# A retention layer and its feed-forward block: the second chunk's recurrence by halves of 64 tokens, with other orders of loads, activations and PSUM tiles

## The chip, the cores and the metric

The kernel runs on one core of one Trainium2 chip. The metric is the device time of one execution in microseconds (us). TensorE (PE) does the matmuls, VectorE (DVE) and ScalarE (ACT) the work on elements, GpSimd (POOL) a few small operations, and SyncE (SP) issues nearly all transfers (DMA), in one queue that is served in order: an instruction that waits holds those behind it.

## The reference

```python
# q, k, v: (B, H, S, D) = (4, 8, 768, 64), fp32
gamma = 1.0 - 2.0 ** (-5.0 - np.arange(H))
for t in range(S):
    state = gamma[None, :, None, None] * state + np.einsum('bhd,bhe->bhde', k[:, :, t], v[:, :, t])
    y[:, :, t] = D ** -0.5 * np.einsum('bhd,bhde->bhe', q[:, :, t], state)
x = y.transpose(0, 2, 1, 3).reshape(3072, 512)
h = x @ w_in                   # (512, 2048)
out = np.maximum(0.01 * h, h) @ w_out      # (2048, 512)
```

The two weight matrices arrive as 64-bit floats and are turned into fp32 on the chip.

## The kernel before

**Chunks.** The 768 tokens are cut into six chunks of `C = 128`; a chunk holds the 128 tokens of all four batches, so 512 rows of x. Decay is taken out of the recurrence: v is multiplied by `gk` ahead of it (`decay_v`, on ACT in the first two chunks, on POOL later) and the result by `gq` behind it (`next_gq` moves `gq` on by one chunk), so that the state itself is a plain sum of k v^T.

**The recurrence in the first two chunks** goes batch by batch over 128 tokens. `score` makes q k^T for the 128 tokens (only the three of four 64 x 64 quarters that are not zero), `masked` (DVE, L211) multiplies by the mask, `reads` (L226) multiplies q with the state, `last_values` and `first_values` (L261, L250) add the scores times v, `state` (L276) makes the new k v^T in the same PSUM tile, `taken` (DVE, L306, L312) copies the result to x times `gq` and adds to the state. In the second chunk two batches go together (`products_together`), and batch 1's scores lie in two banks of the feed-forward pool (`score_apart`, `masked_apart`).

**The recurrence from the third chunk on** (`c >= JOINED`, 2) goes by pairs of batches and by halves of 64 tokens. `scores_of_pair` makes the scores within each half (L369) and the sums k v^T of each half (L380), then on DVE two masked tiles `am` (L387), the state after the first half, `mid`, and the state after the second (both L606, by `plus`). `joint_visit` reads the old state for the first half and `mid` for the second (L427) and adds the scores times v (L444); two POOL memsets (`rows_free`) order matmuls that share rows of the array; four DVE copies (L466) take the result to x, batch 1 of the pair first. For the third chunk both are put between steps of the feed-forward block (`early_scores`, `early_visit`), in a PSUM pool `psum` with two slots of two banks.

**Layout of loads.** Host code lays k and v out token by token; from chunk `JOINED` on, one transfer brings k of both batches of a pair and another v of both (`of_pair`, kind 0 and 1). Tiles with tag "qk" and tag "kv" have two buffers each (`AHEAD`). The last four weight pieces, 28 to 31, use the same buffers for their raw words: even ones "qk", odd ones "kv".

**Feed-forward, first two chunks.** `direct` (L683), `hidden` and `output` (L662) multiply by seven products of 2 x 2 blocks. Each product, and each step of `direct`, is four fp32 matmuls of 128 x 256, which the profile shows as a row of x8: every fp32 matmul is two records. The seven go through four PSUM banks A to D, M1 being copied into bank B by ACT; `differences` makes the sums of x blocks that the products need (t[0] first), `add_sums` and `last_sum` those of the weights. Between the steps the 32 pieces of weights are turned into fp32: `powers` on ACT (three activations), `mantissas` on DVE (L590, L595, L602). `sum_of_unit` and `keep_unit` prepare further sums of weights and store them (`kept`).

**Feed-forward, later chunks.** From 240 us on, `inner` (L1182) does a second level of seven products with the stored weights, read back into `wa` and `wb` (`load_unit`, group 0 and 1), and `outer` puts its results together on DVE and applies the leaky activation on ACT (L1218). `inner` copies products to SBUF on ACT (L1186 to L1194): M3 adds into the bank that held M5, M7 into the one that held M6, so each waits for that copy.

**Order.** The order on each engine is the order of the Python calls (`tc.manual_schedule()`); waits come from the tile framework. Steps of a product are interleaved by hand: `run(steps, {2: [...]})`, `next(steps)`, `products(steps, n)`, and the tables `hidden_more` and `output_more`, whose key `s3` means "after step 3".

## Time and profile before

| | us |
|---|---|
| profiled execution | 644.66 |
| its span, first to last instruction | 642.9 |
| six runs: 644.66, 645.28, 646.89, 642.82, 642.52, 642.72; median | 643.74 |
| PE busy in the span | 631.7 (98%) |
| DVE busy | 462.6 (72%) |
| ACT busy | 269.5 (42%) |
| POOL busy | 22.7 (4%) |

A row of the timeline gives the start, the busy time, the engine, the source line, the operation, the tiles written and read, the tile of the array, the shape and the number of records; a bracket tells how long the engine stood before and what ended that. A windows row gives for a stretch the busy time of each engine, then the granted clock of TensorE (1.00 is full), the busy share of the DMA engines and what they moved in GB/s. Ends of matmuls are modelled, so the distance of two starts is a better measure than a busy time.

### The profile page before, as it was taken

The page shows a single profiled execution, that of the slowest core. Times are in us where ns is not written, and L with a number is a line of the kernel's source. Part 1 is how long each engine was busy: PE and PEld are TensorE (multiplying, and loading weights), DVE is VectorE, ACT ScalarE, POOL GpSimd, SP SyncE. Part 2 cuts the span into 40 slices and gives each one's busy share as a digit, 9 for nine tenths or more (in the row PEclk, how much of TensorE's full clock was granted, in tenths as well). Part 3 has the DMA queues.
Part 4 walks back from the last instruction along what each step waited for, and adds up shares of the span by engine and source line. Part 5 has one row for each costly group of instructions (what it writes and reads, how often), then busy time and mean ns, then how long its engine had stood idle before and what let it go on. Part 6 is the DMA issues. An engine that isn't in the chain of part 4 may idle for free.

```text
span 642.9 us, 14287 instructions
## 1 busy us (share of the span) xinstructions
PE 631.7 (98%) x6086; PEld 570.6 (89%) x6086; DVE 462.6 (72%) x760; ACT 269.5 (42%) x515; POOL 22.7 (4%) x45
## 2 busy tenths in 40 slices
PE   8999999999999989999999999999999999999997
PEld 5888888888888879899999999999999999999996
DVE  5689769889979856657876756778637778637655
ACT  5876557257252114352342433523424423533521
POOL 2000000000011010101000001000010000000000
PEclk9999999999999989999999999999999999999999
DMA  8931327455953987384844573844445336545201
GB/s 332 406 120 46 119 66 246 129 198 157 308 220 92 354 308 260 88 295 127 275 133 136 165 228 110 296 161 156 152 151 190 95 115 187 166 150 167 86 1 67
DMA packets 87536, 113.42 MB, mean 176 GB/s; under 512 B 3240, under 2 KB 71720, under 8 KB 87472
## 3 DMA queue, kind: packets, MB, share of 16 engines
q1 hardware_dynamic: 87168, 111.88, 52.7%
q8 instruction: 48, 0.79, 0.5%
q10 hardware_dynamic: 304, 0.62, 0.3%
q14 instruction: 16, 0.13, 0.1%
HBM read 93.35 MB, written 19.14 MB: 175 GB/s over the span
## 4 chain that ended last, share of the span: by engine, by line
PE 88%; DMA 6%; DVE 3%; ACT 2%; issue 1%; SPq 0%; DVEq 0%
PE bank L662 31%; PE bank L1182 27%; PE B_o L662 4%; PE C_o L662 4%; PE A_o L662 4%; PE A_h L662 3%; PE C_h L662 3%; PE B_h L662 3%; DMA qk<-in_qk_dram 2%; PE D_o L662 2%; PE D_h L662 2%; DMA x_words<-in_weights_dram 1%; DMA in<-in_kv_dram 1%; PE bank L444 1%; PE bank L380 1%; PE bank L369 1%
## 5 line engine op out<-in xcount | busy, mean ns | idle before, releaser
L606 DVE TENSOR_TENSOR o<-o,bank 128x512 f32<-128x512 f32 (+2 forms) x91 | 58.6, 662 | 55.0 <-PE bank L662 33.5
L606 DVE TENSOR_TENSOR made<-made,bank 128x512 f32<-128x512 f32 (+1 forms) x96 | 56.4, 619 | 57.0 <-PE bank L1182 52.6
L662 PE MATMUL bank<-g,w 128*128 128x256 f32 x384 | 89.9, 382 | 0.0
L662 PEld LDWEIGHTS bank<-g,w 128*128 128x128 f32 x384 | 70.7, 190 | 9.2
L1182 PEld LDWEIGHTS bank<-x,wb 128*128 128x128 f32 x672 | 77.6, 192 | 0.8
L1182 PE MATMUL bank<-x,wb 128*128 128x128 f32 x672 | 77.6, 275 | 0.0
L1182 PE MATMUL bank<-x,wa 128*128 128x128 f32 x512 | 68.8, 276 | 0.6 <-ACT made L1188 0.6
L662 PE MATMUL bank<-gd,w 128*128 128x256 f32 x288 | 66.1, 379 | 0.0
L1182 PEld LDWEIGHTS bank<-x,wa 128*128 128x128 f32 x512 | 63.8, 192 | 2.4 <-ACT bank L1186 0.8
L662 PEld LDWEIGHTS bank<-gd,w 128*128 128x128 f32 x288 | 54.7, 190 | 7.4
L1182 PE MATMUL bank<-t,wa 128*128 128x128 f32 x384 | 53.3, 275 | 0.0
L1218 ACT ACTIVATE g<-g 128x512 f32<-128x512 f32 x64 | 39.5, 632 | 31.5 <-DVE g L606 31.5
L1182 PEld LDWEIGHTS bank<-t,wa 128*128 128x128 f32 x384 | 48.0, 192 | 0.0
L1186 ACT COPY bank<-bank 128x512 f32<-128x512 f32 (+1 forms) x32 | 16.7, 522 | 67.8 <-PE bank L1182 67.5
L606 DVE TENSOR_TENSOR g<-made 128x512 f32<-128x512 f32 x64 | 42.7, 688 | 1.1
L755 ACT COPY bank<-bank 128x512 f32<-128x512 f32 x17 | 9.7, 570 | 72.4 <-PE bank L662 72.3
L609 DVE TENSOR_TENSOR gd<-g,gd 128x512 f32<-128x512 f32 x48 | 33.2, 692 | 4.9
L773 ACT COPY bank<-bank 128x512 f32<-128x512 f32 x16 | 9.1, 570 | 50.2 <-PE bank L662 50.2
L662 PE MATMUL bank<-g,last 128*128 128x256 f32 x120 | 29.0, 387 | 0.0
L662 PE MATMUL bank<-gd,last 128*128 128x256 f32 (+1 forms) x124 | 27.5, 373 | 0.0
L662 PE MATMUL A_h<-x,w 128*128 128x256 f32 x112 | 26.6, 380 | 0.0
L662 PEld LDWEIGHTS bank<-gd,last 128*128 128x128 f32 x124 | 22.8, 190 | 3.2 <-DVE gd L609 0.3
(223 smaller groups left out, 1030.5 us busy)
## 6 DMA issues: line engine op xcount, KB each, us to landing
wa<-kept SPq DMA_DIRECT2D x16, 1344.0 KB, 8.0
raw<-in_weights_dram SPq DMA_DIRECT2D x31, 512.0 KB, 4.3
wb<-kept SPq DMA_DIRECT2D x16, 896.0 KB, 5.3
wa<-kept SPq DMA_DIRECT2D x16, 448.0 KB, 4.3
wb<-kept SPq DMA_DIRECT2D x16, 448.0 KB, 6.2
out_dram<-o SPq DMA_DIRECT2D x23, 256.0 KB, 3.3
kept<-w SPq DMA_DIRECT2D x12, 448.0 KB, 5.8
qk<-in_qk_dram SPq DMA_DIRECT2D x10, 512.0 KB, 8.2
```

What stands on the lines that cost most here:

```text
L369: nc.tensor.matmul(at[j][ts(h, 64), n, m, i], lhsT=x[ts(j, 64), 1, a, ts(h, 64)], rhs=x[ts(j, 64), 0, a, ts(h, 64)], start=(n == 0 and a = ...
L380: nc.tensor.matmul(sums[h][ts(j, 64), n, a], lhsT=key[ts(h, 64), 2 * a + j], rhs=val[ts(h, 64), 2 * a + j], start=(n == 0 and a == 0), sto ...
L444: mm = nc.tensor.matmul(at[n][j][ts(i, 64), m, ts(h, 64)], lhsT=val[ts(h, 64), 2 * a + j], rhs=weights[j][ts(h, 64), n, m, i], start=(n == ...
L606: nc.vector.tensor_tensor(out=out, in0=a, in1=b, op=ALU.add)
L609: nc.vector.tensor_tensor(out=out, in0=a, in1=b, op=ALU.subtract)
L662: nc.tensor.matmul(to, lhsT=block(w, sa)[:, k, ts(i, 128)], rhs=rhs[:, k, a:z], start=(first and (i == 0 or split) and n == 0 and k == 0), ...
L755: nc.scalar.copy(out=bank_of("B"), in_=ps)
L773: nc.scalar.copy(out=bank_of("D"), in_=ps)
L1182: nc.tensor.matmul(ps[q][:, i], lhsT=w[:, j, i], rhs=part_of(moving[i], s), start=(i == 0 and m in ("M1", "M5", "M4")), stop=True, skip_gr ...
L1186: nc.scalar.copy(out=ps[3], in_=ps[0])
L1218: nc.scalar.activation(g[:, i], g[:, i], AF.Prelu, alpha=0.01)
```

## The change

**Second chunk.** `JOINED` becomes 1, so the second chunk's k and v come by pairs and its recurrence runs through `early_scores` and `early_visit`. `reads`, `score_apart`, `masked_apart`, `products_together` and `scored_later` go. The places where `c > JOINED` stood now read `c > 2`. For each pair the tile with v is loaded ahead of the one with k, and v of both batches is decayed ahead of the pair's sums.

**Loads.** The third chunk's two qk loads move ahead of its v and k; the fourth chunk's likewise, and `load_unit(0, 1)` (`wb`) moves behind them.

**PSUM tiles.** `early_visit` asks for the tile of batch 1 of the pair before that of batch 0.

**Activations.** At the start of the two-level part, `outer(0, 1)` runs its DVE sums ahead of the last output step, and its four leaky activations come in twos after M1 and after M4 of the next inner product instead of all four after M1.

```diff
+    def inputs_into(place, c, b, kind):
+        flat = place.rearrange("p i k n -> p (i k n)")
+        half = 2 * HP * C
+        heads[c, b + kind] = [flat[:, 0:half].rearrange("p (s a t) -> p s a t", s=2, a=HP)]
+        load_qk(c, b + kind)
+        of_pair(c, b, kind, flat[:, half : 2 * half].rearrange("p (n h d) -> p n h d", n=2, h=H))
+        rooms[c, b, kind] = flat[:, 2 * half : 2 * half + 2 * HP * D]
...
     def early_visit(c, b):
         def do():
-            joint_visit(c, b, [pair_of_banks(f"yp{n}_{c}_{b}") for n in range(2)])
+            banks = [pair_of_banks(f"yp{n}_{c}_{b}") for n in (1, 0)]
+            joint_visit(c, b, banks[::-1])
         return do
...
+            load_qk(2, 0)
+            load_qk(2, 1)
             of_pair(2, 0, 1)
             of_pair(2, 0, 0)
-            for b in range(2):
-                load_qk(2, b)
...
-    load(1, 0, unit_tile(LATE[2], "in10"))
-    load(1, 1, unit_tile(LATE[1], "in11"))
+    inputs_into(unit_tile(LATE[2], "in11"), 1, 0, 1)
+    inputs_into(unit_tile(LATE[1], "in10"), 1, 0, 0)
...
-    load(1, 2, unit_tile(LATE[0], "in12"))
+    inputs_into(unit_tile(LATE[0], "in13"), 1, 2, 1)
...
-    load(1, 3)
+    heads[1, 2] = [work.tile([128, 2, HP, C], FP32, tag="qk", bufs=AHEAD, name="qk_1_2")]
+    load_qk(1, 2)
+    of_pair(1, 2, 0)
...
     next(steps)
-    scored_later(0)
     decay_v(1, 1, nc.scalar)
+    early_scores(1, 0, spare(1, 0, 0))()
+    next_powers()
     next(steps)
-    score_apart(1, 1)
-    next_powers()
-    next_mantissas()
-    for j in range(2):
-        masked_apart(1, 1, j)
-    next_powers()
-    products_together(0)
+    early_visit(1, 0)()
     next_mantissas()
     decay_v(1, 2, nc.scalar)
+    decay_v(1, 3, nc.scalar)
     next_powers()
-    decay_v(1, 3, nc.scalar)
-    taken(1, 0, x1)
-    taken(1, 1, x1)
     next(steps)
-    scored_later(2)
-    scored_later(3)
+    early_scores(1, 2, spare(1, 2, 1))()
+    next_mantissas()
     later = hidden(1, 0, x1, t1, *parts[1][1:], order=FIRST)
     next(later)
     last_sum(0)
+    next_powers()
+    early_visit(1, 2)()
     next_mantissas()
-    products_together(2)
     next_powers()
     run(steps, {})
-    tokens_taken(1, 2, x1)
-    tokens_taken(1, 3, x1)
     differences(x1, t1)
     next_gq()
-    state_taken(1, 2, for_state(sums_at[1, 2]))
-    state_taken(1, 3, for_state(sums_at[1, 3]))
...
         load_unit(0, 0)
...
-        load_unit(0, 1)
 
     def next_heads():
+        for b in range(2):
+            ahead(3, b)
         of_pair(3, 0, 1)
         of_pair(3, 0, 0)
-        for b in range(2):
-            ahead(3, b)
...
-                     s3=[early_visit(2, 0), differ(2), next_heads],
+                     s3=[early_visit(2, 0), differ(2), next_heads, lambda: load_unit(0, 1)],
...
     inner(0, 1)
+    later = []
+    outer(0, 1, later)
     products(last, 1)
     begun = inner_steps(1, 0, held=True)
-    products(begun, 1)
-    outer(0, 1)
+    for steps, leakies in ((1, later[:2]), (2, later[2:])):
+        products(begun, steps)
+        for do in leakies:
+            do()
...
-                products(begun, 7)
+                products(begun, 5)
...
-JOINED = 2
+JOINED = 1
```

## The prediction

> **What bounds the kernel now.** I read the page first: TensorE (PE) is busy 98% of the span and the chain that ended last is 88% PE, so only PE's own work and PE's waits count; VectorE (DVE, 72%) and ScalarE (ACT, 42%) matter where PE waits for them. The windows give PE no idle time from 35 to 200 us. So in the second chunk each microsecond of matmuls is one of time. Next the timeline of PE alone. Columns: start, busy, engine, line, tiles, records; every fp32 matmul is two records.

> ```profile
> 25.74 1.89 PE L683 MATMUL d<-x,w 128*128 128x256 f32 x8
> 27.56 0.90 PE L191 MATMUL ap<-in 64*64 64x128 f32 x32
> 28.39 1.99 PE L683 MATMUL d<-x,w 128*128 128x256 f32 x8
> ...
> 44.64 1.99 PE L683 MATMUL d<-x,w 128*128 128x256 f32 x8
> ...
> 48.20 1.03 PE L662 MATMUL C_h<-t,w 128*128 128x256 f32 x4
> ```

> ```profile
> 190.07 1.89 PE L662 MATMUL A_h<-x,w 128*128 128x256 f32 x8
> 191.89 1.16 PE L369 MATMUL ap<-in 64*64 64x64 f32 x64
> 192.87 1.11 PE L380 MATMUL sp<-in,in 64*64 64x64 f32 x64
> 193.92 1.99 PE L662 MATMUL C_h<-t,w 128*128 128x256 f32 x8
> ...
> 199.20 1.89 PE L662 MATMUL A_h<-x,w 128*128 128x256 f32 x8
> ...
> 203.19 1.13 PE L662 MATMUL C_h<-x,w 128*128 128x256 f32 x4
> ```

> The upper rows are the ends of the second chunk's recurrence, which stands between dense blocks; the lower ones are the third chunk's, already by halves: scores and state sums of a pair at 191.89, its visit between 199.20 and 203.19. The distance of two dense starts, less a dense block's 1.73 us, is what an excursion costs, with the gaps where the tile shape changes.

> Then PE's waits. After 186 us the same timeline shows five, and the windows show what one of them does to the clock:

> ```profile
> 209.12 0.69 PE L369 MATMUL ap<-qk 64*64 64x64 f32 x32 [0.48 <-DVE x L466]
> 210.69 0.69 PE L369 MATMUL ap<-qk 64*64 64x64 f32 x32 [0.88 <-DMA qk<-in_qk_dram]
> ...
> 233.99 0.69 PE L369 MATMUL bank<-qk 64*64 64x64 f32 x32 [1.55 <-DMA qk<-in_qk_dram]
> 235.24 0.69 PE L369 MATMUL bank<-qk 64*64 64x64 f32 x32 [0.56 <-DMA qk<-in_qk_dram]
> ...
> 259.86 0.49 PE L1182 MATMUL bank<-x,wa 128*128 128x128 f32 x2 [0.59 <-ACT made L1188]
> ```

> ```profile
> 236.00:240.00 4.00, 4.00 (x71) 3.53 (x66) 2.65 (x4) 0.00 (x0) 0.00 (x0) 0.60 0.41 91
> ```

> The windows row is a stretch, the engines' busy times, and as its last three numbers the granted clock, the DMA share and GB/s: 0.60 after PE stood 2.1 us. Last, SyncE's (SP) own timeline, for why qk was late:

> ```profile
> 202.81 0.33 SPq L136 DMA_DIRECT2D k<-in_kv_dram  x1
> 203.18 1.72 SPq L119 DMA_DIRECT2D qk<-in_qk_dram  x2
> ```

> The qk loads stand behind k, whose room comes free late. 22 us later it is the same again: wb is issued at 219.44, v at 221.55 (its issue took 3.71), k at 225.36 and only then qk at 225.78.

> **Part 1, the second chunk by halves.** From the dense block at 25.74 to C_h at 48.20 before: 22.46 us, of which six dense blocks (25.74, 28.39, 35.41, 38.83, 44.64, 46.48) are 6 x 1.73 = 10.38 and the filling of bank B some 0.32 (38.83 to 40.97, less the 1.82 from block to recurrence). That leaves 11.76 for two pairs. By halves a pair costs 193.92 - 190.07 - 1.73 = 2.12 for scores and sums and 203.19 - 199.20 - 1.73 = 2.26 for the visit (2.12 at 215.81 to 219.66): 4.31, twice 8.62. Ideal gain 3.14. Against it stand new waits:
> - The sums of pair 0 need both batches' decayed values. ACT decays the second from 27.61 to 29.63, behind two leaky activations and next_gq as before; the sums reach it at 28.96 and would end at 29.43, so they end near 29.8: 0.4 lost. Queued behind them on PE is only the dense block.
> - Loads: the order in SP is the same in bytes. Values come first (landed 23.4), the last keys are issued at 18.21 and 24.77; transfers into these tiles landed 7.0 to 10.1 us after issue, so by 28.3 and 34.9, and are needed at 28.5 and 36.5. Cost 0, up to 0.3. ACT decays pair 2 in one go from 31.5 to 35.6, before its sums.
> - DVE: am, am and two states take 2.52 (195.27 to 197.79), the four copies of a visit 1.32 (207.60 to 208.92), a weight piece's mantissas 1.86 (30.88 to 32.74). The first visit ends near 33.8 and from there DVE runs without a gap: copies to 35.0, mantissas to 36.9, pair 2's am and states to 39.4, mantissas to 41.3, last_sum to 41.9, copies to 43.2, mantissas to 45.0 (now ahead of the differences), t[0] to 45.7. C_h wants t[0] at 45.5, so it starts near 45.85, not 45.06 as without any wait: that is 2.35 before 48.20. The states need 39.7 for the second visit, which starts at 39.7: no wait, at most 0.3.
> - The lag of DVE meets one copy of bank B near 58 us: 0.15. DVE's idle time at 69.12 and 74.42 (0.98 and 2.15, waiting for PE and ACT) then gives the rest back, so the lead stays to 186 us, and DVE's chain from 188.61 starts from PE's C_h.
> Taken: 2.2; ends 0.3 (pairs wait 2.8 us more) and 3.1.

> [...] The rows decide: 128 records of the visit at 201.02 to 203.19 take 2.17 us, 17 ns each.

> **Part 2, the third chunk's loads.** At 209: qk(2,0) takes the room of weight piece 28 and is issued before 185.6; qk(2,1) that of piece 30, free at 198.95, some 4 us earlier than now. What they are moved past: v(2,0) now waits behind qk(2,1), is issued near 199.4 rather than 185.56, and with 3.4 to 4.7 us to land is there by 204; POOL's decay (2.54) ends by 206.6, the sums need it at 209.5. The 0.48 goes too: early_visit now takes its banks so that those copied out first, 0.7 us before the others, are the ones the next scores need. So A_o at 206.75 plus 1.73 plus 2.12 gives C_o at 210.60 instead of 212.25: 1.65. Ends 0.9 (only the load's wait goes) and 1.9.

> At 234: qk(3,0), qk(3,1), v, k now stand ahead of wb and are issued as soon as the visit ends (218, on the clock of before less part 1), ahead of wb's 1344 KB. The kept stores ahead of them lose two qk transfers (3.4 us). Behind wa (issued by 214, then 8.0 to landing on the page, so 222) and at 1.3 us per 512 KB (382 to 406 GB/s in the windows from 230 to 236), qk lands by 225, v by 226.5, POOL's decays (2.04) end by 228.6; the scores start at 230.7, the sums 0.9 later. wb lands 4 us after k, near 231.7; its first matmul, 248.23 before, moves to 242.5. The five stores of o follow wb instead of qk; the loads into o's room wait for them and are needed only at 269. Without the wait the dense block at 230.55 is followed by 2.12 of excursion and a block of 1.73 at full clock: L1182 starts at 236.13 instead of 240.25: 4.12. Of this some 1.6 is the halved clock (sums 1.81 for 0.93, dense block 2.67 for 1.92 in the chain of waits). Ends 2.1 (the clock still drops) and 4.2.

> [...] Here 2.1 us of standing sufficed, while 1.36 us at 209 to 211 left 1.00. [...]

> **Part 3, the leaky activations.** At 258.11 ACT runs them ahead of the copy that M3 waits for (0.59). Now two follow M1's copy and two M4's; M5's copy ends at 258.0, M3 wants it at 259.1. M6's copy ends near 260.25, M7 wants it at 260.0. So 0.59 becomes 0.2: 0.4 gained, ends 0 and 0.6. DVE's add into o moves behind five sums; its bank is not written before 269, and the output's transfer has no reader.

> **Sum.** 2.2 + 1.65 + 4.12 + 0.4 = 8.4. The profiled execution took 644.66 (span 642.9, 1.8 around it): 636.3. It lies 0.9 above the median of the six, 643.74; if the waits for qk make that spread, as I take it, the result comes from 636.3, else from 635.4.

> **Rivals.**
> - DVE eats part 1. For: it is without a gap from 34 to 46 in my working, and a mantissa step of 1.86 us now stands ahead of t[0]. Against: its recurrence is no larger (8.2 us in the rows before, 2 x 3.84 = 7.7 after). Part 1 falls to 0.3: 638.2.
> - The late load of the fourth chunk moves, but stays: qk and v wait behind kept and wa, v's decay ends 2 us after the scores want to start, and the clock halves as before. For: v took 9.9 us to land. Against: 3 us of margin above. Part 2 falls to 1.65: 640.4.
> - Slower: the sums of a pair stand in PE's order before a dense block and need both batches' loads and sixteen decays by ACT. If the second pair's loads or ACT come late, PE stands us for us, and beyond 2.1 us the clock adds 1.6. For: DMA is 96% busy to 35 us. From 6.8 us of standing the run is slower than before; with 10 us it is 644.66 - 8.4 + 11.6 = 647.9. Against: pair 2's values are issued at 20.92 and so there by 31.0, 0.5 before ACT asks for them.
> - The change doesn't do what it says: the order of instructions shows the quarters, loads and activations where the diff has them; left out.

> **How the numbers follow.** Forecast 0.65, DVE 0.18, late load 0.13, slower 0.04. The low end, 634.0, is the upper ends of all parts (9.8) off the median of the six; the high end, 640.2, leaves out the slower case and most of the late load. A change of 0.5% (3.2 us) is about what a measurement can tell: faster 0.92 (forecast, DVE and nearly all of the late load), same 0.05, slower 0.03.

> **What would show it.** C_h's start near 45.9 (right) or above 47.5 (DVE); no PE wait for qk near 207 and 227; clock 1.00 between 225 and 240; no wait for ACT's copy above 0.3 near 252. A PE wait above 1 us for anything in 27 to 45 us, or for v or wb near 228 to 245, makes it wrong.

## The result and the profile after

| | before | after |
|---|---|---|
| median of the runs side by side, us | 644.52 (47 runs, 642.13 to 648.05) | 640.00 (21 runs, 639.08 to 641.92) |
| ratio | | 0.9934, 95% interval 0.9922 to 0.9947 |
| profiled execution, its span | 644.66, 642.9 | 640.17, 638.4 |
| start of C_h in the second chunk | 48.20 | 49.24 |
| start of L1182, L1126 after | 240.25 | 235.92 |

By the ratio the kernel is 0.66% faster, by the medians 4.5 us, where 8.4 were forecast. The 640.0 lies inside the range, at its upper end. The page of the kernel after, its engines' line, one of its DMA queues, and the chain that ended last:

```profile
PE 629.5 (99%) x6214; PEld 568.1 (89%) x6214; DVE 462.5 (72%) x763; ACT 269.4 (42%) x515; POOL 22.7 (4%) x45
...
q8 instruction: 49, 0.80, 0.5%
...
PE 96%; DMA 1%; DVE 1%; ACT 1%; issue 1%; SPq 0%; DVEq 0%
```

DMA's share of the chain falls from 6% to 1%, and the waits for qk are gone. The second line becomes important below (packets, MB, share); before it read:

```profile
q8 instruction: 48, 0.79, 0.5%
```

The later stages of PE's timeline, for the rows before at 209 to 240, and the windows for the clock:

```profile
207.95 1.89 PE L628 MATMUL A_o<-g,last 128*128 128x256 f32 x8
209.77 1.16 PE L334 MATMUL ap<-qk 64*64 64x64 f32 x64
211.81 1.99 PE L628 MATMUL C_o<-gd,last 128*128 128x256 f32 x8
...
231.93 1.16 PE L334 MATMUL bank<-qk 64*64 64x64 f32 x64
235.92 0.38 PE L1126 MATMUL bank<-x,wa 128*128 128x128 f32 x2
```

```profile
235.00:240.00 5.00, 5.00 (x43) 4.87 (x42) 3.46 (x7) 2.57 (x5) 0.00 (x0) 1.00 0.66 213
```

Scores in one row without a bracket: no wait for qk at either place, and the clock is 1.00. But the second chunk is late. Its rows, and all the waits of PE there that are new:

```profile
24.00 0.46 PE L238 MATMUL yp<-am,in 64*64 64x64 f32 x16 [0.66 <-issue]
...
28.04 1.16 PE L334 MATMUL ap<-in 64*64 64x64 f32 x64
...
29.02 0.65 PE L345 MATMUL sp<-in,in 64*64 64x64 f32 x31
...
31.44 0.73 PE L345 MATMUL sp<-in,in 64*64 64x64 f32 x33 [1.76 <-issue]
32.10 1.99 PE L649 MATMUL d<-x,w 128*128 128x256 f32 x8
...
44.23 0.40 PE L392 MATMUL yp<-in,states 64*64 64x64 f32 x12 [0.63 <-issue]
...
49.24 1.10 PE L628 MATMUL C_h<-t,w 128*128 128x256 f32 x4 [0.20 <-ACT dec L100]
```

"issue" says that PE stood and the profile shows nothing that it waited for. The first stands in the last rows of the first chunk, ahead of the recurrence that was changed; the other two stand in the middle of a group of equal matmuls, the longest after 31 of the 64 records of pair 0's sums. ACT's decays, which the prediction named for that place, were over at 30.10; PE went on at 31.44. A bracket with "issue" on the engine that bounds the kernel is the thing to follow.

**What PE waited for.** q8 carries instructions, by its name on the page. It made 49 fetches of 16.4 KB (16,384 bytes each in the trace; 0.80 MB in all). The trace has 12,428 matmuls and weight loads and 94 other instructions of TensorE: 12,522 / 49 is 255.6 for each fetch, so 256 with the last one not full, 64 bytes an instruction. Before it was 12,263 in 48, 255.5. So I take q8 to bring PE's own instructions in blocks of 256. In order of start, with its semaphore instructions, those ahead of which PE stood are the 706th, 962nd and 1730th: 256, and three times 256, apart. So each is the first of a block. The same count holds in every profile of this case: PE stood 0.25 us or more without a releaser 26 times between its first and its last matmul, in eleven profiled executions, and each time the instruction behind the wait is the 194th plus a multiple of 256. No other wait of that length is without a releaser. The DMA view of the kernel after shows when the block that began at 31.44 was fetched. From 24.00, where the block ahead of it began, to 28.9 the engines are full (DMA share 1.03) and q8 has no packet; then it has its one:

```profile
DMA packets 550, 2.02 MB, mean 412 GB/s; under 512 B 57, under 2 KB 57, under 8 KB 550
...
q1 hardware_dynamic: 550, 2.02, 103.3%
```

```profile
q8 instruction: 1, 0.02, 5.7%
```

The first fence is 24.0 to 28.9, the second a row of 28.9 to 30.1. The trace puts the fetch at 28.99 and its end at 30.09; PE went on 1.35 us after that. The same reading for the other two waits: fetch ended at 22.64, PE on at 24.00 (1.36); 42.92 and 44.23 (1.30). So theory F: a block of 256 is fetched at about the time when PE comes to the block ahead of it; the fetch stands behind the loads that fill the DMA engines (it began 5.0 us here after PE began the block ahead; 0.66 and 1.03 behind 285.88 and 35.31, where the DMA share was 0.00); 256 short matmul instructions, 128 records, last 2.2 us (the visit at 202.23 to 204.40 takes 2.17), so the next block isn't there. In the kernel before, PE began the block ahead at 23.52; the fetch ended at 29.56, so by the 1.35 above the next block could be used at some 30.91. PE, with its 128-token matmuls, was through the block ahead only at 31.59: 0.7 us of margin that nobody saw.

### The profile page after: what moved, and what is told of

It reads as the page before. It is cut to its first block, busy times and chain, and to the rows that moved or that the text cites. A ratio compares the mean times of both kernels' runs of the same rounds, so it can differ in the third digit from the quotient of the medians.

```text
span 638.4 us, 14552 instructions
## 1 busy us (share of the span) xinstructions
PE 629.5 (99%) x6214; PEld 568.1 (89%) x6214; DVE 462.5 (72%) x763; ACT 269.4 (42%) x515; POOL 22.7 (4%) x45
## 4 chain that ended last, share of the span: by engine, by line
PE 96%; DMA 1%; DVE 1%; ACT 1%; issue 1%; SPq 0%; DVEq 0%
PE bank L628 32%; PE bank L1126 27%; PE C_h L628 4%; PE B_o L628 4%; PE A_o L628 4%; PE C_o L628 4%; PE B_h L628 4%; PE A_h L628 4%; PE d L649 2%; PE D_o L628 2%; PE D_h L628 2%; DMA raw<-in_weights_dram 1%; PE bank L334 1%; PE bank L409 1%; PE bank L392 1%; PE bank L345 1%
## 5 line engine op out<-in xcount | busy, mean ns | idle before, releaser
L1126 PEld LDWEIGHTS bank<-x,wb 128*128 128x128 f32 x672 | 77.6, 192 | 0.8
L1126 PE MATMUL bank<-x,wb 128*128 128x128 f32 x672 | 77.6, 275 | 0.0
L1126 PE MATMUL bank<-x,wa 128*128 128x128 f32 x512 | 68.7, 276 | 0.1
L1126 PEld LDWEIGHTS bank<-x,wa 128*128 128x128 f32 x512 | 63.8, 192 | 1.8 <-ACT bank L1130 0.8
L1126 PE MATMUL bank<-t,wa 128*128 128x128 f32 x384 | 53.4, 275 | 0.0
L1168 ACT ACTIVATE g<-g 128x512 f32<-128x512 f32 x64 | 39.4, 632 | 30.8 <-DVE g L572 30.8
L1126 PEld LDWEIGHTS bank<-t,wa 128*128 128x128 f32 x384 | 48.0, 192 | 0.0
L628 PE MATMUL bank<-g,last 128*128 128x256 f32 x120 | 28.3, 380 | 0.0
```

Source lines behind the costliest of these rows:

```text
L628: nc.tensor.matmul(to, lhsT=block(w, sa)[:, k, ts(i, 128)], rhs=rhs[:, k, a:z], start=(first and (i == 0 or split) and n == 0 and k == 0), ...
L1126: nc.tensor.matmul(ps[q][:, i], lhsT=w[:, j, i], rhs=part_of(moving[i], s), start=(i == 0 and m in ("M1", "M5", "M4")), stop=True, skip_gr ...
L1168: nc.scalar.activation(g[:, i], g[:, i], AF.Prelu, alpha=0.01)
```

## The experiments

Rivals to F: A, the sums wait for decayed values or loads; D, DVE's chain bounds the second chunk; R, chance; later T, transfers of one kernel.

**The parts alone.** The first is the kernel before with the second and third part of the change, its second chunk as it was; in the other only the second chunk is changed. Lines of the first one's edit:

```diff
+            banks = [pair_of_banks(f"yp{n}_{c}_{b}") for n in (1, 0)]
+            joint_visit(c, b, banks[::-1])
...
+            load_qk(2, 0)
+            load_qk(2, 1)
             of_pair(2, 0, 1)
             of_pair(2, 0, 0)
...
+        for b in range(2):
+            ahead(3, b)
         of_pair(3, 0, 1)
         of_pair(3, 0, 0)
...
+    later = []
+    outer(0, 1, later)
```

> The kernel before with the second and third part of the change alone (order of loads, PSUM tiles, leaky activations); its second chunk's recurrence stays as before. Theory F (part 1 costs time, because PE's instructions are fetched too slowly for its short matmuls; parts 2 and 3 gain what was forecast): 1.65 + 3.9 + 0.25 = 5.8 us faster than before, so about 638.5 us and faster than the changed kernel by 1.2 us. Rival D (part 1 gains as forecast and the loss lies in later stages): 6 us less gain than that here, or about 642 us, slower than the changed kernel.

638.88 us, ratio 0.9942 (0.9926 to 0.9958). The trace: C_h 48.24, A_o 206.76, C_o 210.62, L1182 234.78, with no PE wait above 0.4 from 14 us on. As F says.

> The changed kernel with the second and third part undone, so that only the second chunk's recurrence by halves is left. Theory F: PE waits in the sums of pair 0 (1.8 us) and in the visits without any releaser, C_h starts near 49.2 us, and the kernel is 1 us slower than before, 645.5. Rival D: C_h starts near 46 and the kernel is 2 us faster, 642.5.

644.89 us beside 643.32 of before, ratio 1.0025 (1.0002 to 1.0049): part 1 alone costs time. The profiled execution was the slowest of twelve, 650.21. The waits of 1.76, 0.62 and 0.48 are at the same matmuls. C_h starts at 50.39, later than expected: the clock was 0.50 from 33 to 35 us after the wait of 1.76, which it was not in the profiled execution of the change.

**Fewer loads under way.** In the trace of the change SP lets each load wait for the eighth before it (the one at 17.12 for that of 7.39, by their semaphore); here for the third or the second, from the second chunk's first load to its last.

```diff
+    def paced(load):
+        if len(issued) >= 3 and pacing[0]:
+            tc.add_manual_dep(load.ins, issued[-3].name, IN_ORDER, reason="pace of the loads")
+        issued.append(load.ins)
...
-        nc.sync.dma_start(out=raws[n], in_=weights[n])
+        paced(nc.sync.dma_start(out=raws[n], in_=weights[n]))
```

> The changed kernel, in which each of SP's loads of the second chunk and of the weight pieces between them waits until the third load before it has landed, so that at most three are under way. Theory F with its cause (an instruction fetch of PE stands behind the transfers that are queued in the DMA engines, 5.0 us at 24 us): the fetches at 21.5 and 29.0 start 1 to 2.5 us earlier, the waits of 0.66 and 1.76 shrink to 0 to 0.5 together, one of up to 1 us may come in the first visit, and C_h starts near 47.5 to 48; 1 to 2 us faster than the changed kernel. Rival A (the wait in the sums is for ACT's decays or for the pair's loads): loads land no earlier or later, so the wait stays at 1.8 us or grows, and the time is that of the changed kernel or longer.

> As the run before, with at most two loads under way. Theory F: the fetches start earlier still (delay 1.3 to 2.5 us behind the block's first instruction), no wait in the sums of pair 0; but the loads may lose bandwidth and land 1 to 3 us later, which PE would then wait for by name (DMA) in pair 1 or in the pieces' conversion. Rival A: later loads make the wait in the sums longer than 1.8 us.

The fetch behind 23.3 us starts 2.5 us after PE began the block ahead with three loads under way and 1.7 with two, instead of 5.0. Both kernels have no wait on "issue" left in the second chunk. PE's rows with three:

```profile
27.35 1.16 PE L343 MATMUL ap<-in 64*64 64x64 f32 x64
28.33 1.46 PE L354 MATMUL sp<-in,in 64*64 64x64 f32 x64
...
33.66 1.99 PE L658 MATMUL d<-x,w 128*128 128x256 f32 x8
36.88 0.69 PE L343 MATMUL ap<-qk 64*64 64x64 f32 x32 [1.23 <-DMA qk<-in_qk_dram]
...
38.96 1.34 PE L354 MATMUL sp<-in,k 64*64 64x64 f32 x64 [0.92 <-DMA k<-in_kv_dram]
...
48.33 1.97 PE L637 MATMUL C_h<-t,w 128*128 128x256 f32 x8 [0.21 <-DVE t L584]
```

The sums of pair 0 come in one row of 64. A falls: the loads land later and the wait goes all the same. But the DMA engines are no longer full (80% busy from 23.3 to 25.7 us), pair 1's qk and k come late, and PE now waits for them by name. 639.25 us, ratio 0.9946 (0.9931 to 0.9961). C_h comes 0.91 us earlier than in the change; in all 1 to 2 us were expected, and the gain is not shown: the median is 0.75 us lower, but the two were not run side by side, and the changed kernel's ratio is 0.9934. With two loads qk is 5.98 us late: 647.48 us.

**The change again, and other queues.** Four loads under way, and both depths with weight piece 6 loaded behind pair 1's qk and k.

```diff
-        if n != 3:
+        if n not in (2, 3):
             load_piece(n + 4 if n < 3 else n + 3)
...
     of_pair(1, 2, 0)
+    load_piece(6)
```

> The changed kernel again, beside the next three. Theory F: the waits of 0.66, 1.76 and 0.63 without a releaser are there again within 0.2 us, since the position of the instruction blocks and the queued transfers are the same; about 640 us. Rival R (these waits are chance): they are elsewhere or of another length.

> The changed kernel with at most four loads under way until the second chunk's last one is issued (three starved the DMA engines: pair 1's qk and k came 1.2 and 0.9 us late). Theory F: the fetch behind 24 us starts 2.5 to 4 us after the block's first instruction instead of 5.0; the wait in the sums of pair 0 is 0 to 1.0 us, pair 1's loads come in time or up to 1 us late; C_h near 47.5 to 48.5, 638.5 to 639.5 us.

> At most three loads under way as in the run with three, and piece 6 of the weights is loaded behind pair 1's qk and k instead of ahead of them (1.3 us each earlier). Theory F: no wait without a releaser in 23 to 33 us; the waits of 1.23 for qk and 0.92 for k shrink to 0 to 0.4; C_h near 46.4 to 47.2, where the forecast's own sum would have it but for the loads; 637.3 to 638.5 us, faster than before, than the changed kernel and than the kernel with the second and third part alone. Rival D (DVE's chain bounds part 1): C_h stays at 48 or later, with a wait for t, although PE stands no more ahead of it.

> The same order with at most four loads under way. Theory F: waits without a releaser of up to 1 us, no wait for qk or k; C_h near 46.4 to 47.5; 637.3 to 638.8 us.

| run | waits on "issue", 23 to 46 us | other waits for loads | C_h | C_h less these waits | median us |
|---|---|---|---|---|---|
| the change, profiled | 0.66, 1.76, 0.63 | | 49.24 | 46.19 | 640.00 |
| the change again | 1.76, 0.31, 0.36 | | 48.87 | 46.44 | 639.96 |
| three loads | none | 1.23, 0.92 | 48.33 | 46.18 | 639.25 |
| four loads | 1.22, 1.13, 0.27 | | 49.18 | 46.56 | 640.69 |
| three, other order | 1.00, 1.52 | | 48.82 | 46.30 | 640.27 |
| four, other order | 0.68, 1.49, 1.13, 0.44 | | 50.03 | 46.29 | 640.94 |

The wait of 1.76 is not chance: it is there again to 0.01 us, though the 0.66 is gone, the 0.63 is 0.36, and 0.31 in the first visit is new. The three kernels with other queues stood 1.2 to 2.1 us above the upper ends of their expected times: once the second pair's loads are in time, PE comes to the next block sooner and stands there (at 39.76, in pair 1's sums, with three loads and the other order). In these runs a wait for instructions that was shortened in one place came back in the next. A pair is two blocks (256 records, 512 instructions), and from PE's start of one block to the use of the next it took 7.4 us in the change while the engines were full (24.00 to 31.44: 5.0 + 1.10 + 1.35); with idle engines some 3 is an estimate (0.66 + 0.92 behind 285.88, and the 1.35 from above). In all of these the wait for instructions ended 1.2 to 1.7 us after the fetch's last byte.

**The blocks moved, nothing else.** 64 more instructions in front, at 2 us.

```diff
-    keep_busy(10)
+    keep_busy(7)
+    for _ in range(35):
+        nc.tensor.matmul(idle[:, 0, 0:64], lhsT=nothing, rhs=nothing[:, 0:64], start=True, ...)
```

> The changed kernel with 64 more TensorE instructions in front (35 narrow matmuls on zeros for three of the ten wide ones that keep PE busy at 2 us), so that every block of 256 instructions begins 64 earlier in the program. Theory F: the wait that came after 31 of the 64 records of pair 0's sums comes ahead of the first of them (62 instructions earlier) and lasts 0.8 to 1.7 us; the one in the second visit moves from the middle of a group of reads to a place 64 instructions ahead, in the values or the first reads; the first visit gets one of 0.5 to 2 us. Together they stay near 2.5 us, and so does the time, 640 us within 1. Rival A (the wait is for decayed values or loads): it stays at the same matmul, after 31 records.

```profile
28.70 1.23 PE L345 MATMUL sp<-in,in 64*64 64x64 f32 x64
...
34.83 0.38 PE L409 MATMUL yp<-am,in 64*64 64x64 f32 x9 [2.00 <-issue]
```

The data are the same, and the sums of pair 0 run through, where 0.8 to 1.7 us of waiting ahead of them were expected: PE began the block ahead 1.6 us earlier (22.37 for 24.00), the fetch ended at 27.07, so by the 1.35 above the block could be used at some 28.4; the sums began at 28.70. The wait is now in the first visit, 2.00 us, 64 instructions ahead of where the change has its next block. The second visit has no wait above 0.25, where one was expected. A is out for good. The time, 640.75 us, stays within 1.

**Fewer bytes.**

```diff
+        if n in (4, 5, 6):
+            nc.gpsimd.memset(raws[n].bitcast(U32)[:, 64:], 0)
+            nc.sync.dma_start(out=raws[n][:, 0:32], in_=weights[n][:, 0:32])
+            return
```

> The changed kernel with a sixteenth of the bytes of weight pieces 4, 5 and 6 loaded (the rest of their words is set to zero on POOL), which takes some 3.7 us of transfers out of the stretch from 22 to 33 us. Theory F: the fetch that started 5.0 us after its block's begin starts within 3.5; the waits without a releaser between 23 and 36 us shrink from 2.1 to 0.6 or less in sum; C_h starts at 46 to 46.8 instead of 49. Rival D: C_h stays above 47.5 and waits for DVE or ACT.

> The kernel before with the same three pieces cut to a sixteenth, as a control. Theory F: nothing to gain, C_h stays at 48.2 within 0.3, so that the run with the change is ahead by 1.4 to 2.2 us at C_h, the forecast of part 1 (2.2). Rival D: C_h moves as far as in the run with the change, and part 1 gains nothing even so.

A miss: 638.95 us (ratio 0.9925) with the change, 644.80 (1.0017) without. With the change the fetch still starts 4.82 us after PE began the block ahead and PE still stands 1.64 and 0.45; C_h is at 48.00. SP issued the loads of the chunk no earlier than in the changed kernel (the last, k, at 25.18 for 24.35), and the engines were still full from 24 to 28 us (DMA share 1.06 in the windows), when the fetch was waiting; only from 28 to 32 did the share fall, to 0.41. So this run doesn't test part 1 without contention, as it was meant to, and why fewer loads under way shorten the fetch's wait while fewer bytes did not is left open. C_h of the control stayed, at 48.27, but the lead of 1.4 to 2.2 us at C_h that was expected over it is 0.27.

**Half of it, and the same half with other blocks.** Pair 0 by whole batches as before, pair 1 by halves; then the same with 80 instructions in front (`keep_busy(7)` and 43 narrow matmuls).

```diff
-    early_scores(1, 0, spare(1, 0, 0))()
...
-    early_visit(1, 0)()
+    scored_later(0)
...
+    products_together(0)
...
+    taken(1, 0, x1)
+    taken(1, 1, x1)
```

> The changed kernel with pair 0 of the second chunk (batches 0 and 1) by whole batches as before, and pair 1 alone by halves; second and third part of the change as they are. Theory F: pair 0 needs 352 instructions less... of the short kind than by halves only in part, but its fetches had a margin of 0.7 us before, so no wait above 0.3 there; pair 1 stands after the loads have landed and its second visit waits 0 to 0.6; C_h at 46.8 to 47.7; 637.3 to 638.5 us, faster than before, than the changed kernel, and than the kernel with the second and third part alone. Rival D: C_h at 48 or later.

> The mixed kernel (pair 0 by whole batches, pair 1 by halves) with 80 more TensorE instructions in front, so that each block of 256 begins 80 earlier; nothing else differs. Theory F: the wait of 1.00 at 45.1 and that of 4.40 at 222.6 vanish or fall to 0.5 at most, for the block that was late there is asked for before the visit instead of within it, and with them the halved clock of 220 to 230; C_h near 47.3; 638.0 us within 0.7, 9 us less than the mixed kernel. Rival T (the wait of 4.40 belongs to the transfers or buffers of the mixed kernel): it stays at the same matmul, and the time near 647.

The mixed kernel took 647.29 us (twelve runs, 641.12 to 648.51), ratio 1.0039 (1.0016 to 1.0062), some 9 us above what was expected; C_h came at 48.33, where 46.8 to 47.7 were. It stood 1.00 us at 45.10, and some 175 us later, in code that the edit does not touch, 4.40 us. Its last rows of the third chunk's second visit, and the clock after them:

```profile
217.56 0.63 PE L449 MATMUL yp<-am,v 64*64 64x64 f32 x29
222.60 0.48 PE L449 MATMUL yp<-am,v 64*64 64x64 f32 x3 [4.40 <-issue]
```

```profile
220.00:225.00 5.00, 2.40 (x8) 1.92 (x8) 1.82 (x4) 0.00 (x0) 0.00 (x0) 0.64 0.89 344
```

The block ahead began at 215.37, the fetch began at 220.13 with qk and v under way and full engines, and ended at 221.24, and PE went on 1.36 later. With the blocks 80 earlier, the same visit's last row and the same stretch, in two fences:

```profile
217.11 0.65 PE L449 MATMUL yp<-am,v 64*64 64x64 f32 x32
```

```profile
220.00:225.00 5.00, 5.00 (x25) 4.22 (x24) 4.74 (x9) 0.00 (x0) 0.00 (x0) 1.00 1.03 397
```

638.86 us, ratio 0.9920 (0.9897 to 0.9943) for 1.0039: 8.4 us less by the medians, 7.7 by the ratios (the two were not run side by side), for 80 instructions in front, with the same transfers. T falls. (C_h is at 47.72, not 47.3, and the time 0.2 above the expected range.) The place of the blocks alone is worth more here than the whole change. This run also shows pair 1 by halves without a wait for instructions or loads, from the dense block ahead of its scores to C_h:

```profile
35.66 1.99 PE L689 MATMUL d<-x,w 128*128 128x256 f32 x8
...
47.72 1.97 PE L668 MATMUL C_h<-t,w 128*128 128x256 f32 x8 [0.21 <-ACT dec L101]
```

**Side by side.**

> The kernel before with the second and third part alone, again, beside the other two. Theory F: 638.9 us within 0.5, some 1 us less than the changed kernel in the same comparison.

> The changed kernel again, beside the other two: 640.0 us within 0.5; the wait of 1.76 in the sums of pair 0 for the third time.

638.78 us (638.61 to 639.22) without part 1, 640.64 (639.45 to 642.04) with it: no run of the one reaches those of the other. So part 1 costs 1 to 2 us, and the kernel with the second and third part alone, ratio 0.9915 (0.9892 to 0.9938) against before, beats both kernels. The mixed one with 80 in front is not told apart from it. The last run's profile had waits of 1.81 and 0.98, and the first was followed by this:

```profile
31.00:33.00 2.00, 2.00 (x37) 1.66 (x38) 1.27 (x2) 1.93 (x8) 0.00 (x0) 0.70 0.89 348
33.00:35.00 2.00, 2.00 (x6) 1.20 (x4) 0.10 (x1) 2.00 (x10) 0.00 (x0) 0.50 0.15 61
35.00:37.00 2.00, 2.00 (x125) 1.87 (x128) 0.00 (x0) 1.94 (x5) 0.20 (x2) 0.95 0.00 0
```

Half the clock for a dense block (3.61 us busy for 1.99) costs 1.6 us more. In the other two profiled executions of the change a wait of 1.76 left the clock at 1.00. That is probably why the changed kernel spreads: of the 22 executions listed with its result, the six of 640.8 us or more have a mean clock of 0.997, the others 0.999 or 1.000.

## Why the prediction was right or wrong

**Part 1, the failing step.** "Against it stand new waits" listed ACT, loads, DVE and a PSUM copy, and left out PE's own instructions: their price was put at nothing without a reason. 2.2 us of gain were forecast; C_h came 1.04 late instead. The terms one by one:
- The ideal of 3.14 and the price of the rows hold. The visit in the run with three loads takes 33.66 - 31.64 = 2.02 us, 16 ns a record. But the 17 ns a record came from short bursts with no wait on "issue" in them. For a rate that lasts, the fetch has to keep up: in the change the fetches at 21.53 and 28.99 lay 7.46 us apart, with the engines full from 24.0 to 28.9. One block, 128 records, in 7.4 us is my estimate of what can be had there.
- ACT's decays, 0.4: right. Where no instruction is missing the sums of pair 0 take 29.71 - 28.33 = 1.38 from start to start, instead of 193.92 - 192.87 = 1.05 in the third chunk: 0.33. In the change PE stood 1.76 there, past the end of the decays.
- Loads, 0: right, pair 1's came in time.
- DVE, 0.4: t[0] is indeed last at C_h (0.2). In the change's profile the bracket names ACT's `dec`, which ended within 0.02 us of t; with three loads C_h starts at 48.33 while that step still runs, until 49.02. The table above gives 46.2 to 46.6 for C_h without the waits for instructions and loads, against 45.85 in the working. That is worked out from six profiles, not shown in one.
- Each pair was free of both kinds of waits once, in different kernels. Pair 0 with three loads takes 33.66 - 27.35 = 6.31 us from its scores to the dense block behind its visit, 35.41 - 27.56 = 7.85 before: 1.54 less. Pair 1 in the mixed kernel with 80 in front takes 47.72 - 35.66 = 12.06, 48.20 - 35.41 = 12.79 before: 0.73 less. Together that is 2.27, where the working had 2.35 at C_h. So the terms it had are borne out for PE; that DVE would have kept up with both pairs is not shown, since in the mixed kernel it has the mantissas of two weight pieces less between the two pairs' copies to x.
- Missing: 0.66 + 1.76 + 0.63 = 3.05, and sometimes a halved clock. The 0.66 lies ahead of the second chunk and was not there in the other two profiled executions of the change, so it comes and goes and is no price of the halves; the 1.76 and the waits in the visits are. That the second chunk stood 0.17 later still at 191 us has no cause that I tested.

"No idle time from 35 to 200 us" was read as: here only matmuls count. It held for the matmuls of before. Pair 0 lies mostly ahead of 35 us, where the DMA engines are full (share 0.98 from 25 to 35), and there the fetch had 0.7 us to spare.

**Part 2: right.** At 209: A_o to C_o is 211.81 - 207.95 = 3.86 against 5.50 before, 1.64 for the forecast 1.65. At 234: from the dense block at 230.11 to L1126 5.81 us against 9.70, 3.89 for 4.12. The clock stayed at 1.00 there, as the sum had it.

**Part 3: half.** From L1126 to the end the kernel gained 0.2 us of the 0.4. The wait for ACT's copy went; PE waits 0.18 for `made` at 257.61 instead.

**The sum.** Forecast -2.2 - 1.65 - 4.12 - 0.4 = -8.4; spans measured +1.04 + 0.17 - 1.64 - 3.89 - 0.2 = -4.5.

That 640.0 falls inside the range is luck: its high end made room for a late load, not for instructions.

**The rivals.** The rival nearest in time, the late load of the fourth chunk (640.4), did not happen. "DVE eats part 1" gave 638.2, and its sign, C_h above 47.5, was seen; its mechanism was not, since PE stood where DVE's work was not what it waited for. The slower rival named the place, a wait in pair 0's sums, with the wrong cause, and its 6.8 us were not reached. The text had said what would make it wrong, a PE wait above 1 us in 27 to 45 us, and that is where it failed.

## What to carry to other kernels

Count the instructions of a stretch as well as its microseconds: a change to shorter matmuls needs PE's blocks of 256 sooner, and where the DMA engines were full a block could be used only 7.4 us after PE began the one ahead (24.00 to 31.44). A wait put down to "issue", often in the middle of equal matmuls, with the instruction queue's packet 1.2 to 1.7 us ahead of its end, was that in all 26 cases here. Before a kernel is judged by a few microseconds, move its blocks by some tens of instructions in front: here that was worth some 8 us in one kernel, most of it in code that its edit never touched, and nothing clear in another (640.75 for 640.00).
